# A fused retention and MLP kernel: batch 0's queries and keys loaded four tokens a partition by head pair

## The chip, the cores and the metric

The kernel runs on one core of a Trainium2 chip. The time is device microseconds of one launch; a kernel's time is the median of its runs. A profiled execution has a time of its own, and a span: from its first to its last instruction.

## The reference

```python
# q, k, v: (8, 8, 576, 64) float32   w_in: (512, 2048)   w_out: (2048, 512)
scores = q @ k.T / sqrt(64)                          # per batch and head
gamma  = 1 - 2 ** (-5 - h)                           # per head
ret    = scores * where(i >= j, gamma ** (i - j), 0)
x      = (ret @ v), heads side by side               # (8 * 576, 512)
out    = gelu_tanh(x @ w_in) @ w_out                 # (4608, 512)
```

The mask depends on the difference of positions alone, so the attention can be cut into chunks: scores inside a chunk of 128 tokens, and a 64 by 64 state per head that carries what came before.

## The kernel before

**Tiles.** A batch has 512 tokens in four chunks, and 64 tail tokens, which have a path of their own (`Tt`, `kqt`, `vt`). The number `s` is the half of 256 tokens, `hh` the half of four heads. `load_qkv(b, s, hh, key)` brings 256 KB into a tile of 128 partitions by 512 float32: partition p has tokens 2p and 2p + 1 of the half, for four heads, so each run in memory is 512 bytes. `cast_qk` (the copies all have line L232) makes float16 of it in the order token, head, feature, in `kq[:, s, hh, i, :]`, where i is 0 for keys and 1 for queries. `cast_v` (L241) does so for values and folds a decay into them.

**Attention of a batch.** `tr` transposes 128 by 128 blocks of `kq` on TensorE (L342) into a PSUM bank and copies them (L232 again) into `T`, whose index g = 2r + pp stands for token parity r and head pair pp. When its engine is written `S2`, ScalarE takes one half of the copy and VectorE the other. `score_mm` (L395) multiplies transposed keys and queries; `mask_sc` (L408, VectorE) applies the mask on the way out of PSUM, into `ret`. `state_mm` (L463) multiplies the natural keys in `kq` with the values; `scan` (L479, L483, VectorE) carries the state on from chunk to chunk, and `put` (L232) writes it into block-diagonal tiles `tbd`, which `tbd_zero` (L132) cleared. `values` (L510) is `ret` times values, `inter_mm` (L537) adds the state's part for chunk n = 2s + c, and `evac` (L550, VectorE) scales the sum into `x`.

**The MLP.** `up` (L598) and `up_half` (L684) multiply `w_in` and x, and ScalarE applies the gelu (L602, L690). `up_half(j, u)` needs half u of x alone, and all four row blocks of its column group of `w_in`, cast to float16 by `cast_w_in`. The down-projection (`product`, L740) forms seven products of mixed operands ("my" to "mz2") in place of eight; the sums and differences that they need are made by `mix_sa`, `mix_sc`, `mix_d` (L701, L709, L713), for the weights by `mix_w_out` (L323 to L331), and `settle` (L767) puts the results together. In the last two blocks (the tail rows of all batches, then batch 7), some up-projections go the same way (`pair_*`, with `forms_w` and `forms_x`).

**The order.** All loads go out on SP's queue, in the order of the `load_*` calls, from line 860 on. A load needs one of 12 slots, or a tile on loan (E, E2, E3, O, H); a slot comes free when the cast of what it held is issued in program order, and SP then waits for that cast. The order of all else is a list of units (mostly one up-projection or down-product each) and a plan: entries (unit, step), run after that unit, in the order of the list. The first ten units are empty, so all of batch 0's attention stands there. Each engine runs its own instructions in this order and waits at each for what it needs. `pads` gives the number of filler transposes or matmuls (L147, L149) that TensorE runs ahead of a step while it has nothing else, and `warm` (L138) fills its first microseconds.

Of the kernel before, what the change touches and what calls it, by code (L numbers as in the profile page):

```python
# [13 lines left out]
F16 = mybir.dt.float16  # L14
# [5 lines left out]
def kernel(  # L20
# [106 lines left out]

    tbd = [const.tile([128, NC, HP, 128], F16, name=f"tbd{i}") for i in range(2)]
# [56 lines left out]
    def load_qkv(b, s, hh, key, home=None):  # L185
        def one(home):
            t = ld(home)
            nc.sync.dma_start(  # L188
                out=t.rearrange("p (h e) -> p h e", h=4),
                in_=SRC[key][b, 4 * hh : 4 * hh + 4, 256 * s : 256 * s + 256, :].rearrange(  # L190
                    "h (p r) d -> p h (r d)", r=2
                ),
            )
            att[b][key, s, hh] = t

        todo.append((one, home))
        pump()
# [36 lines left out]
    def cast_qk(b, s, hh, key, eng):  # L234
        t = att[b].pop((key, s, hh))
        copy(eng, unperm(att[b]["kq"][:, s, hh, "kq".index(key), :]), perm(t))
        done(t)
# [99 lines left out]
    def tr(b, s, hh, i, eng):  # L337
# [3 lines left out]
        for g in range(4):  # L341
            nc.tensor.transpose(t[:, 128 * g : 128 * g + 128], a["kq"][:, s, hh, i, 128 * g : 128 * g + 128], ident)  # L342
        src = t[:, 0:512].rearrange("p (g t) -> p g t", g=4)
# [34 lines left out]
    def tr_tail_dma(b):  # L378
        a = att[b]
        nc.sync.dma_start_transpose(  # L380
            out=a["Tt"].rearrange("p i s t -> p (i s) t"),
            in_=a["kqt"].rearrange("p i c -> p (i c)"),
        )

# [463 lines left out]
    def add(plan, *entries):  # L848
# [12 lines left out]
    load_qkv(0, 0, 0, "q", None)  # L861
    load_qkv(0, 0, 1, "k", None)
    load_qkv(0, 0, 0, "v", None)
    load_qkv(0, 0, 1, "q", None)
    load_qkv(0, 1, 0, "k", None)
    load_qkv(0, 0, 1, "v", None)
    load_qkv(0, 1, 1, "k", None)
    load_qkv(0, 1, 0, "q", None)
    load_w_in(0, 3, E)
    load_qkv(0, 1, 1, "q", None)  # L870
    load_qkv(0, 1, 0, "v", None)
    load_w_in(0, 0, E)
    load_qkv(0, 1, 1, "v", None)
    load_w_in(0, 2, E)
    load_w_in(0, 1, E)
    load_w_in(1, 1, E2)
    load_w_in(1, 0, E2)
    load_w_in(1, 3, E2)
    load_w_in(2, 2, None)
    load_qkv(1, 0, 0, "k", None)  # L880
    load_w_in(1, 2, E2)
    load_w_in(2, 3, None)
    load_w_in(2, 0, None)
    load_qkv(1, 0, 1, "q", None)
    load_w_in(2, 1, None)
    load_qkv(1, 0, 0, "q", None)
    load_qkv(1, 0, 1, "k", None)
    load_w_in(3, 0, None)
# [3 lines left out]
    load_w_in(3, 2, None)  # L892
    load_qkv(1, 0, 1, "v", None)
    load_qkv(1, 1, 0, "k", O)
    load_qkv(1, 1, 1, "q", O)
    load_qkv(1, 1, 0, "q", O)
    load_qkv(1, 1, 1, "k", O)
# [5 lines left out]
    load_w_out(2, None)  # L903
    load_w_out(3, None)
    load_w_out(10, H)
    load_w_out(4, E3)
# [3 lines left out]
    load_w_out(13, H)  # L910
    load_w_out(7, E3)
    load_w_out(9, O)
# [3 lines left out]
    load_w_out(12, H)  # L916
    load_qkv(2, 1, 0, "q", None)
    load_qkv(2, 1, 0, "k", None)
    load_qkv(2, 0, 0, "k", None)
    load_qkv(2, 0, 0, "q", None)  # L920
# [8 lines left out]
    load_tail(0)  # L929
    load_qkv(3, 0, 0, "v", None)  # L930
    load_qkv(3, 0, 0, "k", None)
    load_qkv(3, 0, 0, "q", None)
# [13 lines left out]
        ("tr", 0, 1, 0, 0): 0,  # L946
        ("tr", 0, 1, 1, 0): 0,
        ("tr", 0, 1, 1, 1): 5,
        ("st", 0, 1, 0): 6,
        ("st", 0, 1, 1): 11,  # L950
        ("us", 0, 0): 0,
        ("us", 0, 1): 8,
        ("xs", 0, 0): 1,
        ("xs", 0, 1): 2,
# [3 lines left out]
        ("tr", 0, 0, 1, 0): 24,  # L958
        ("tr", 0, 0, 1, 1): 9,
        ("st", 0, 0, 0): 12,  # L960
        ("st", 0, 0, 1): 7,
        ("us1", 0, 0): 3,
        ("tr", 0, 1, 0, 1): 6,
        ("in", 0, 1): 12,
        ("us1", 0, 1): 1,
        ("in", 0, 2): 4,
# [6 lines left out]
    def turn():  # L973
# [7 lines left out]
    plan = add({},  # L981
        (0, L(tbd_zero, 0, G)),
        (0, L(cast_qk, 0, 0, 0, "q", G)),
        (0, L(cast_qk, 0, 0, 0, "k", G)),
        (0, L(mask)),
        (0, L(tr, 0, 0, 0, 1, A)),
        (0, L(cast_v, 0, 0, 0, G)),
        (0, L(tr, 0, 0, 0, 0, S2)),
        (0, L(score_mm, 0, 0, 0)),
        (1, L(cast_qk, 0, 0, 1, "k", V)),  # L990
        (1, L(tr, 0, 0, 1, 0, A)),
        (3, L(mask_sc, 0, 0, 1)),
        (5, L(tbd_zero, 1, G)),
        (0, L(cast_v, 0, 0, 1, G)),
        (1, L(mask_sc, 0, 0, 0)),
        (1, L(cast_qk, 0, 0, 1, "q", V)),
        (1, L(tr, 0, 0, 1, 1, V)),
        (3, L(state_mm, 0, [0])),
        (2, L(score_mm, 0, 0, 1)),
        (3, L(cast_qk, 0, 1, 0, "q", G)),  # L1000
        (0, L(cast_qk, 0, 1, 0, "k", G)),
        (3, L(scan, 0, 0)),
        (3, L(put, 0, 0, A)),
        (6, L(cast_qk, 0, 1, 1, "q", G)),
        (0, L(new_x, 0)),
        (4, L(scan, 0, 1)),
        (5, L(evac, 0, 0, 0)),
        (4, L(tr, 0, 1, 0, 0, V)),
        (3, L(values, 0, 0)),
        (4, L(tr, 0, 1, 0, 1, S2)),  # L1010
        (5, L(cast_qk, 0, 1, 1, "k", A)),
        (4, L(put, 0, 1, A)),
        (6, L(score_mm, 0, 1, 0)),
        (5, L(inter_mm, 0, 0, 1)),
        (5, L(evac, 0, 0, 1)),
        (8, L(cast_w_in, 0, 0, V)),
        (6, L(tr, 0, 1, 1, 0, A)),
        (7, L(mask_sc, 0, 1, 0)),
        (7, L(cast_v, 0, 1, 0, G)),
        (7, L(score_mm, 0, 1, 1)),  # L1020
        (6, L(tr, 0, 1, 1, 1, A)),
        (7, L(cast_v, 0, 1, 1, V)),
        (8, L(scan, 0, 2)),
        (7, L(state_mm, 0, [1])),
        (7, L(mask_sc, 0, 1, 1)),
        (8, L(put, 0, 2, V)),
        (8, L(cast_w_in, 0, 1, G)),
        (3, L(cast_w_in, 0, 3, A)),
        (9, L(cast_w_in, 0, 2, G)),
        (9, L(F0.up_half, 0, 0)),  # L1030
        (10, L(F0.up_half, 1, 0)),
        (8, L(values, 0, 1)),
        (9, L(evac, 0, 1, 0)),
        (12, L(cast_w_in, 1, 0, G)),
        (9, L(inter_mm, 0, 1, 1)),
        (15, L(cast_w_in, 2, 3, G)),
        (9, L(evac, 0, 1, 1)),
        (8, L(inter_mm, 0, 1, 0)),
        (8, L(turn)),
        (9, L(cast_w_in, 1, 3, A)),  # L1040
        (12, L(cast_qk, 1, 0, 0, "k", G)),
        (15, L(cast_qk, 1, 0, 1, "k", A)),
        (7, L(cast_w_in, 1, 2, A)),
        (11, L(scan, 0, 3)),
        (11, L(F0.mix_sa, 0, 2, V)),
        (14, L(F0.mix_sc, 0, 2, V)),
        (10, L(cast_w_in, 1, 1, V)),
        (10, L(cast_w_in, 2, 2, G)),
        (14, L(cast_w_in, 2, 1, A)),
        (10, L(cast_w_in, 2, 0, V)),  # L1050
        (19, L(F0.mix_sc, 2, 2, V)),
        (16, L(cast_qk, 1, 0, 1, "q", G)),
        (16, L(cast_qk, 1, 0, 0, "q", G)),
        (16, L(F0.mix_d, 0, 2, V)),
        (19, L(tr, 1, 0, 1, 0, V)),
        (18, L(cast_w_in, 3, 0, G)),
        (16, L(tr, 1, 0, 0, 0, S2)),
        (11, L(put, 0, 3, A)),
        (17, L(cast_w_in, 3, 2, G)),
        (19, L(tr, 1, 0, 1, 1, A)),  # L1060
        (20, L(F0.mix_sa, 2, 2, V)),
        (17, L(tr, 1, 0, 0, 1, S2)),
        (20, L(score_mm, 1, 0, 0)),
        (21, L(F0.mix_d, 2, 2, V)),
        (27, L(inter_mm, 1, 0, 0)),
        (21, L(cast_v, 1, 0, 1, G)),
        (22, L(mask_sc, 1, 0, 1)),
        (18, L(cast_w_in, 3, 1, A)),
        (16, L(cast_v, 1, 0, 0, G)),
        (21, L(mask_sc, 1, 0, 0)),  # L1070
        (18, L(cast_w_in, 3, 3, G)),
        (21, L(score_mm, 1, 0, 1)),
        (26, L(scan, 1, 1)),
        (22, L(state_mm, 1, [0])),
        (21, L(new_x, 1)),
        (26, L(cast_qk, 1, 1, 0, "k", G)),
        (22, L(scan, 1, 0)),
        (22, L(put, 1, 0, A)),
        (22, L(values, 1, 0)),
        (23, L(inter_mm, 1, 0, 1)),  # L1080
        (27, L(cast_v, 1, 1, 0, V)),
        (23, L(evac, 1, 0, 1)),
        (28, L(put, 1, 1, A)),
        (22, L(cast_qk, 1, 1, 1, "q", A)),
        (25, L(cast_qk, 1, 1, 0, "q", G)),
        (22, L(cast_qk, 1, 1, 1, "k", A)),
        (28, L(F0.mix_sa, 4, 2, V)),
        (28, L(F0.mix_sc, 4, 2, V)),
        (27, L(cast_v, 1, 1, 1, V)),
        (22, L(evac, 1, 0, 0)),  # L1090
        (25, L(tr, 1, 1, 0, 1, A)),
        (28, L(tr, 1, 1, 0, 0, V)),
        (26, L(tr, 1, 1, 1, 1, A)),
        (28, L(state_mm, 1, [1])),
        (28, L(F0.mix_d, 4, 2, V)),
        (28, L(tr, 1, 1, 1, 0, A)),
        (31, L(mask_sc, 1, 1, 0)),
        (31, L(mask_sc, 1, 1, 1)),
        (28, L(score_mm, 1, 1, 0)),
        (32, L(inter_mm, 1, 1, 1)),  # L1100
        (29, L(score_mm, 1, 1, 1)),
        (31, L(values, 1, 1)),
        (30, L(mix_w_out, 0, "sums", G)),
        (29, L(scan, 1, 2)),
        (29, L(put, 1, 2, A)),
        (31, L(inter_mm, 1, 1, 0)),
        (31, L(mix_w_out, 0, "sub", V)),
        (30, L(mix_w_out, 1, "copy", A)),
        (37, L(mix_w_out, 3, "add", G)),
        (31, L(mix_w_out, 1, "add", V)),  # L1110
        (32, L(mix_w_out, 2, "sums", G)),
        (31, L(mix_w_out, 1, "sums", G)),
        (32, L(evac, 1, 1, 0)),
        (33, L(evac, 1, 1, 1)),
        (33, L(mix_w_out, 3, "sub", V)),
        (37, L(mix_w_out, 7, "add", V)),
        (37, L(mix_w_out, 3, "sums", V)),
        (32, L(mix_w_out, 3, "copy", A)),
        (33, L(mix_w_out, 1, "sub", V)),
        (32, L(mix_w_out, 2, "add", G)),  # L1120
        (38, L(mix_w_out, 0, "copy", A)),
# [390 lines left out]
```

## Time and profile before

| what | us |
|---|---|
| median of 6 runs | 299.55 |
| lowest and highest run | 298.75, 301.22 |
| profiled execution | 299.48 |
| its span | 297.7 |
| TensorE busy in it | 289.1 |
| VectorE busy | 237.1 |
| ScalarE busy | 164.0 |
| GpSimd busy | 104.9 |

Instructions are told by engine (PE for TensorE, PEld for its weight loads, DVE for VectorE, ACT for ScalarE, POOL for GpSimd, SP for SyncE, which issues the DMAs) and by the line of the kernel. A tile of the form `a<-b` is written from b. Matmuls are pipelined, so the length of a row is not a matmul's share of the engine, and a busy TensorE includes filler. TensorE's granted clock is full in the whole span.

### The profile page before, as it was taken

How to read it: one execution, taken by the hardware profiler on the slowest of the kernel's cores; microseconds unless marked ns; L12 is line 12 of the kernel's file. 1: busy time of each engine (PE TensorE's matmuls, PEld its weight loads, DVE VectorE, ACT ScalarE, POOL GpSimd, SP SyncE). 2: the span in 40 equal slices, each digit the busy share in tenths (PEclk: the TensorE clock that was granted, in tenths of full speed). 3: DMA queues.
4: the chain of work that ended last, by engine and by line, in shares of the span. 5: the costliest groups of instructions: out<-in, count | busy, mean ns of one | idle time of the engine just before them, and what ended most of it. 6: DMA issues, size and time to landing. Idle time of an engine off the chain costs nothing.

```text
span 297.7 us, 8946 instructions
## 1 busy us (share of the span) xinstructions
PE 289.1 (97%) x3761; PEld 210.0 (71%) x3761; DVE 237.1 (80%) x442; ACT 164.0 (55%) x318; POOL 104.9 (35%) x136
## 2 busy tenths in 40 slices
PE   8979999999999999999999999999999999999994
PEld 6866477888885568655875587558754886787684
DVE  3795899999997995798568756899688198896793
ACT  7428798875556781665445554564445317605720
POOL 6743664545250433280064005699000000310050
PEclk9999999999999999999999999999999999999999
DMA  7999999858889999979994998482120002002204
GB/s 207 305 327 330 303 380 329 233 143 202 230 240 226 323 231 221 293 221 132 265 259 127 140 254 249 138 140 23 47 98 0 2 34 112 0 2 70 70 2 141
DMA packets 94711, 52.48 MB, mean 176 GB/s; under 512 B 38352, under 2 KB 88528, under 8 KB 94672
## 3 DMA queue, kind: packets, MB, share of 16 engines
q1 hardware_dynamic: 94336, 51.26, 65.5%
q10 hardware_dynamic: 336, 0.66, 0.8%
q8 instruction: 29, 0.48, 0.7%
q14 instruction: 10, 0.08, 0.1%
HBM read 36.70 MB, written 9.44 MB: 155 GB/s over the span
## 4 chain that ended last, share of the span: by engine, by line
PE 71%; DMA 12%; DVE 9%; SPq 3%; ACT 3%; issue 1%; POOL 0%; DVEq 0%; ACTq 0%
PE hp L598 26%; PE my L740 9%; PE mz L740 9%; PE mu L740 5%; PE mw L740 5%; PE mv L740 4%; PE hp L684 2%; PE py L628 2%; DMA loan<-in_q_dram 2%; SPq L188 2%; DMA ld<-in_moe_w_in_dram 2%; DMA ld<-in_v_dram 2%; PE xs L510 2%; DVE ret L408 2%; DVE ost L767 2%; DMA loan<-in_moe_w_in_dram 2%
## 5 line engine op out<-in xcount | busy, mean ns | idle before, releaser
L598 PE MATMUL hp<-x,w_in_sb 128*128 128x512 f16 x400 | 92.4, 379 | 0.6 <-ACT gT L602 0.5
L602 ACT ACTIVATE gT<-hp 128x512 f16<-128x512 f32 x108 | 63.8, 598 | 42.1 <-PE hp L598 41.1
L598 PEld LDWEIGHTS <-w_in_sb 128*128 128x128 f16 x432 | 40.9, 98 | 43.3 <-issue 1.0
L740 PEld LDWEIGHTS <-gT 128*128 128x128 f16 x576 | 55.7, 98 | 8.3 <-ACT gT L671 0.2
L232 POOL CAST kq<-ld 128x512 f16<-128x512 f32 x30 | 23.0, 769 | 60.6 <-DMA ld<-in_k_dram 45.9
L408 DVE TENSOR_TENSOR ret<-st,cm 128x512 f16<-128x512 f32 x64 | 39.9, 679 | 3.7 <-PE st L395 3.5
L241 POOL TENSOR_TENSOR cv<-ld,sc 128x512 f16<-128x512 f32 x28 | 30.3, 1093 | 29.1 <-DMA ld<-in_v_dram 28.9
L232 ACT CAST tbd<-ws 64x256 f16<-64x256 f32 x62 | 25.0, 403 | 25.2 <-DVE ws L483 21.7
L740 PE MATMUL my<-w_out_sb,gT 128*128 128x256 f16 x288 | 34.6, 273 | 0.0
L740 PE MATMUL mz<-w_out_sb,gT 128*128 128x256 f16 x288 | 34.4, 273 | 0.0
L713 DVE TENSOR_TENSOR gT<-gT 128x1024 f16<-128x1024 f16 x34 | 30.8, 918 | 0.2
L740 PEld LDWEIGHTS <-gsum 128*128 128x128 f16 x288 | 28.0, 98 | 3.5
L709 DVE TENSOR_TENSOR gsum<-gT 128x1024 f16<-128x1024 f16 x36 | 29.7, 828 | 0.5 <-ACT gT L602 0.5
L701 POOL TENSOR_TENSOR gdia<-gT 128x512 f16<-128x512 f16 x2 | 3.0, 1482 | 71.0 <-ACT gT L602 49.3
L550 DVE TENSOR_TENSOR x<-xs,gx 128x512 f16<-128x512 f32 x32 | 21.6, 682 | 4.7 <-PE xs L537 4.5
L701 DVE TENSOR_TENSOR gdia<-gT 128x512 f16<-128x512 f16 (+1 forms) x32 | 18.4, 574 | 4.9 <-ACT gT L671 2.5
L767 DVE TENSOR_TENSOR ost<-ost,mv 128x512 f32<-128x512 f32 x18 | 11.5, 678 | 11.6 <-issue 8.1
L684 PE MATMUL hp<-x,w_in_sb 128*128 128x256 f16 x160 | 18.9, 273 | 1.0 <-DVE x L550 0.9
L684 PEld LDWEIGHTS <-w_in_sb 128*128 128x128 f16 x160 | 15.3, 98 | 3.1 <-issue 1.3
L740 PE MATMUL mu<-w_out_sb,gsum 128*128 128x256 f16 x144 | 17.2, 272 | 0.2 <-DVE ret L408 0.2
L740 PE MATMUL mv<-w_out_sb,gsum 128*128 128x256 f16 x144 | 17.2, 273 | 0.0
L740 PE MATMUL mw<-w_out_sb,gdia 128*128 128x256 f16 x144 | 17.2, 273 | 0.0
(113 smaller groups left out, 405.6 us busy)
## 6 DMA issues: line engine op xcount, KB each, us to landing
ld<-in_k_dram SPq DMA_DIRECT2D x30, 256.0 KB, 5.0
ld<-in_q_dram SPq DMA_DIRECT2D x30, 256.0 KB, 5.4
ld<-in_v_dram SPq DMA_DIRECT2D x30, 256.0 KB, 5.5
out_dram<-ost SPq DMA_DIRECT2D x14, 512.0 KB, 4.5
loan<-in_moe_w_out_dram SPq DMA_DIRECT2D x12, 256.0 KB, 5.4
loan<-in_moe_w_in_dram SPq DMA_DIRECT2D x8, 256.0 KB, 6.0
ld<-in_moe_w_in_dram SPq DMA_DIRECT2D x8, 256.0 KB, 6.2
ld<-in_moe_w_out_dram SPq DMA_DIRECT2D x4, 256.0 KB, 5.2
```

The source lines that it names most:

```text
L232: (eng.copy if eng is nc.scalar else eng.tensor_copy)(out=out, in_=in_)
L241: eng.tensor_tensor(out=unperm(att[b]["v"][:, s, hh, :]), in0=perm(t), in1=sc[:, 8 * hh : 8 * hh + 8] .rearrange("p (r h) -> p r h", r=2) ...
L408: nc.vector.tensor_tensor(out=x.rearrange("p (a m) -> p a m", a=2), in0=st[hl].rearrange("p (a m) -> p a m", a=2), in1=cm.rearrange("p r s ...
L550: nc.vector.tensor_tensor(out=xb[b][:, :, 2 * s + c].rearrange("p s q i -> p q s i"), in0=att[b]["x", s][c].rearrange("p (q s i) -> p q s ...
L598: nc.tensor.matmul(hp, w_in_sb[:, ct, 128 * f : 128 * f + 128], x[:, :, ct, :], start=(ct == 0), stop=(ct == 3),)
L602: nc.scalar.activation(out=self.g(f // 2)[:, f % 2], in_=hp, func=AF.Gelu_apprx_tanh)
L684: nc.tensor.matmul(hp[:, 256 * h : 256 * h + 256], w_in_sb[:, ct, 256 * j + 128 * h : 256 * j + 128 * h + 128], xb[self.b][:, :, 2 * u : 2 ...
L701: e.tensor_tensor(out=self.sa[:, j : j + n], in0=g[:, :, 0, 0:256], in1=g[:, :, 1, 256:512], op=ALU.add)
L709: e.tensor_tensor(out=self.sc[:, j : j + n], in0=g[:, :, 0], in1=g[:, :, 1], op=ALU.add)
L713: e.tensor_tensor(out=g.rearrange("p j h c -> p j (h c)")[:, :, 256:768].rearrange("p j (h c) -> p j h c", h=2), in0=g[:, :, :, 0:256], in ...
L740: nc.tensor.matmul(t[u] if isinstance(t, list) else t[:, 256 * u : 256 * u + 256], lhs(j, slice(128 * u, 128 * u + 128)), w_out_sb[:, j, w ...
L767: nc.vector.tensor_tensor(out=out, in0=in0, in1=t, op=op)
```

## The change

Queries and keys of batch 0 (the set `R4`) are loaded with four tokens a partition for a pair of heads over all 512 tokens: runs of 1,024 bytes, and `s` now numbers the pair within the head half. The cast orders them by token and head. After the transposes, column p of block r is token 4p + r; two copies for each `tr`, which step through PSUM with an inner stride of 256 elements, put the tokens into the layout that `T` had. So `T` is as before, but the natural keys in `kq` are not: `back` transposes `T` to natural keys again, for `state_mm`. Scores of a head half now need the tiles of both pairs.

The loads, the pads and the plan are reordered for it, and the plan of batch 1 and of the last two blocks is changed as well.

```diff
+    R4 = {(0, "k"), (0, "q")}
 def load_qkv ... one(home):
+            if (b, key) in R4:
+                g = 2 * (2 * hh + s)
+                nc.sync.dma_start(
+                    out=t.rearrange("p (h e) -> p h e", h=2),
+                    in_=SRC[key][b, g : g + 2, 0:M0, :].rearrange("h (p r) d -> p h (r d)", r=4),
+                )
+                att[b][key, s, hh] = t
+                return
 def cast_qk
-        copy(eng, unperm(att[b]["kq"][:, s, hh, "kq".index(key), :]), perm(t))
+        o = att[b]["kq"][:, s, hh, "kq".index(key), :]
+        if (b, key) in R4:
+            copy(eng, o.rearrange("p (r h d) -> p r h d", r=4, h=2), t.rearrange("p (h r d) -> p r h d", r=4, h=2))
+        else:
+            copy(eng, unperm(o), perm(t))
 def tr
+        if (b, "kq"[i]) in R4:
+            src = t[:, 0:512].rearrange("p (q r s m) -> p s r m q", q=2, r=2, s=2)
+            for r in range(2):
+                e = (A, V)[r] if eng is S2 else eng
+                copy(
+                    e,
+                    a["T"][:, :, hh, i, 2 * r + s, :].rearrange("p s (m q) -> p s m q", q=2),
+                    src[:, :, r],
+                )
+            return
+    def back(b, s, hh, eng):
+        a = att[b]
+        t = bank("tr", F16)
+        pad(("bk", b, s, hh), t)
+        for r in range(2):
+            for pp in range(2):
+                o = 256 * r + 128 * pp
+                nc.tensor.transpose(t[:, o : o + 128], a["T"][:, s, hh, 0, 2 * r + pp, :], ident)
+        copy(eng, a["kq"][:, s, hh, 0, :], t[:, 0:512])
```

The loads of batch 0 before: k and q of (s, hh) = (0, 0), k (0, 1), v (0, 0), q (0, 1), k (1, 0), v (0, 1), k (1, 1), q (1, 0), a weight, q (1, 1), v (1, 0), a weight, v (1, 1), two weights. After: k, q (0, 0), k, q (1, 0), k, q (0, 1), q, k (1, 1), v (0, 1), v (0, 0), a weight, v (1, 0), v (1, 1), three weights.

The plan after, units 0 to 9, for the steps of batch 0 (arguments: batch, s, hh or chunk, k = 0 or q = 1, engine; A is ScalarE, V VectorE, G GpSimd):

```python
(0, cast_qk 0,0,0 q A) (0, cast_qk 0,0,0 k V) (0, cast_qk 0,1,0 q V) (0, tr 0,0,0,0 V) (0, cast_qk 0,1,0 k A) (0, mask)
(0, cast_qk 0,0,1 k A) (0, tbd_zero 0 G) (1, tr 0,0,0,1 V) (1, tr 0,1,0,0 V) (1, tr 0,1,0,1 S2) (1, cast_qk 0,1,1 q G)
(1, cast_qk 0,1,1 k G) (2, score_mm 0,0,0) (2, mask_sc 0,0,0) (2, back 0,0,0 V) (2, cast_qk 0,0,1 q G) (2, tr 0,0,1,0 S2)
(2, tr 0,0,1,1 A) (3, score_mm 0,1,0) (3, back 0,1,0 A) (3, tr 0,1,1,1 V) (3, mask_sc 0,1,0) (3, tr 0,1,1,0 A)
(3, cast_v 0,0,0 G) (3, cast_v 0,0,1 G) (4, score_mm 0,0,1) (4, mask_sc 0,0,1) (5, back 0,0,1 A) (5, state_mm 0,[0])
(5, scan 0,0) (5, values 0,0) (5, scan 0,1) (5, put 0,1 A) (5, evac 0,0,0) (6, score_mm 0,1,1) (6, put 0,0 A)
(6, mask_sc 0,1,1) (6, cast_w_in 0,3 A) (7, back 0,1,1 A) (7, cast_v 0,1,1 V) (7, cast_v 0,1,0 G) (7, state_mm 0,[1])
(7, scan 0,2) (7, put 0,2 S2) (7, values 0,1) (7, tbd_zero 1 G) (7, cast_w_in 1,0 1,3 1,2 A) (8, inter_mm 0,0,1)
(8, evac 0,0,1) (8, inter_mm 0,1,1) (8, inter_mm 0,1,0) (8, cast_w_in 0,1 0,0 G) (8, cast_w_in 1,1 A) (9, cast_w_in 0,2 G)
(9, evac 0,1,0) (9, evac 0,1,1) (9, up_half 0,0) (9, up_half 1,0), then units 10 and 11: up_half 0,1 and 1,1
```

Before, `up_half(0, 0)` stood at unit 9 ahead of `evac(0, 1, 0)`, and `evac(0, 0, 1)` at unit 5. In the last two blocks, `mix_d(0)` and `mix_sa(6)` move from GpSimd to VectorE, and some lists are sorted by unit.

## The prediction

> **What bounds the kernel now.** I read the page first (busy shares, slices, chain), then TensorE's waits, then the timeline of the first 28 us.
>
> The page: busy time; in slices of 7.4 us, TensorE, VectorE and DMA; the chain by engine.
>
> ```profile
> PE 289.1 (97%) x3761; PEld 210.0 (71%) x3761; DVE 237.1 (80%) x442; ACT 164.0 (55%) x318; POOL 104.9 (35%) x136
> PE   8979999999999999999999999999999999999994
> DVE  3795899999997995798568756899688198896793
> DMA  7999999858889999979994998482120002002204
> PE 71%; DMA 12%; DVE 9%; SPq 3%; ACT 3%; issue 1%; POOL 0%; DVEq 0%; ACTq 0%
> ```
>
> TensorE is nearly full from the fourth slice on, so a time is set by two things: when its dense stretch starts, and what it loses afterwards. The 12% of DMA in the chain lie before 46 us: the loads run without a pause, but that is not yet a loss of TensorE's. Its waits from 22.3 to 60 us say so (waiter, awaited: us in total, times, longest):
>
> ```profile
> PE hp L684 <- DVE x L550: 0.9, 1, 0.9
> PE us L463 <- POOL cv L241: 0.4, 1, 0.4
> PE xs L510 <- DVE ret L408: 0.3, 1, 0.3
> ```
>
> After the first line only 0.7 us are left to win before 60 us. That first line is the end of batch 0's attention. The timeline (start, length, engine, operation, idle before it and what ended it):
>
> ```profile
> 6.57 0.29 DVE L232 COPY T<-tr 128x256 f16<-128x256 f16 x1 [3.58 <-ACT T L232]
> 7.21 1.51 PE L147 MATMUL tr<-ident,wz 128*128 128x128 f16 x24
> 9.71 0.43 DVE L232 COPY T<-tr 128x512 f16<-128x512 f16 x1 [0.77 <-PE tr L342]
> 10.64 1.29 DVE L408 TENSOR_TENSOR ret<-st,cm 128x512 f16<-128x512 f32 x2 [0.51 <-PE st L395]
> 12.35 0.82 ACT L232 CAST tbd<-ws 64x256 f16<-64x256 f32 x2 [2.78 <-POOL kq L232]
> ...
> 19.88 1.04 PE L684 MATMUL hp<-x,w_in_sb 128*128 128x256 f16 x8
> 20.97 1.29 DVE L550 TENSOR_TENSOR x<-xs,gx 128x512 f16<-128x512 f32 x2
> 22.31 2.78 PE L684 MATMUL hp<-x,w_in_sb 128*128 128x256 f16 x24 [0.92 <-DVE x L550]
> ```
>
> TensorE's first useful up-projection is at 19.88 us (8 matmuls, a step of 0.87 us); it then waits for x and is dense from 22.31 us. Had those 8 stood in line with the rest, the stretch would begin at 22.31 - 0.87 = **21.44 us**. That is the number to beat. TensorE is "busy" earlier too, but much of that is filler (L147, L149: 24 of them took 1.51 us). What decides is VectorE's queue, busy 4.83 of 5 us before 20 us, while the loads ran at (stretch; busy us of PE, PEld, DVE, ACT, POOL; clock; DMA share; GB/s):
>
> ```profile
> 5.00:10.00 5.00, 5.00 (x95) 4.51 (x92) 2.54 (x6) 2.02 (x5) 1.66 (x3) 1.00 1.13 301
> 15.00:20.00 5.00, 4.44 (x125) 3.82 (x126) 4.83 (x10) 1.53 (x3) 1.96 (x3) 1.00 1.02 345
> ```
>
> The first row is q, k, v in runs of 512 B; the second has mostly weights in runs of 2 KB.
>
> **What the Trainium skill says.** "VectorE: DVE Perf Modes", section "Mode 2×_1P": two 16-bit elements a cycle need elements next to each other in memory. The trace agrees for today's PSUM copies: 512 elements take 422 ns, 256 take 291 ns, so 0.51 ns an element, where the 32-bit masks (L408) take 1.04 if the same fixed 0.15 us is taken off their 684 ns. "DMA: Bandwidth & Descriptors", section "Why small descriptors are slow (HBM only)": a fixed 3 cycles a packet beside its 32-byte beats; so 19 cycles for 512 B and 35 for 1 KB, 8% less a byte. The two rows above (301 and 345 GB/s) go the same way. "TensorE: Matmul & The Clock Gate", section "Part 4: PE-mode transpose": a transpose ends in PSUM and needs a copy after it; here every L342 group has its L232 copy.
>
> **The change, part by part.**
>
> *Loads.* Eight 256 KB loads go from 512 packets to 256. By the 8% above and the two rows I take 0.08 us off 0.86 us each: -0.65 us on the stream after the eighth, -0.3 us at the fourth. In the DMA issue view the fourth load now is issued at 2.32 and lands 5.0 us later, at 7.3 us; it will be at about 7.0. Bounds: nothing, or -1.1 us if the dip in DMA traffic between 3.6 and 5.2 us goes too. Nothing after 22 us waits for the stream for more than the 0.36 us of one GpSimd value cast, so on TensorE I count these savings only through the fourth load. On SP the first 16 loads are the same set in another order, all into free slots or loans, so none waits there; the later ones keep number and size and are costed at nothing while the stream stays ahead of TensorE. If that cover went, the 0.36 us would grow by what they come late.
>
> *What the first scores need.* A tile now holds one head pair over all 512 tokens, so scores of either token half need four loads, not two. VectorE, which reaches its first transpose copy at 6.57 us today, has the cast of the fourth load second in its queue: it starts at 7.0, and the copies behind it wait though their transposes are done.
>
> *PSUM copies.* Each of 8 `tr` calls makes two copies of 256 elements whose inner step is 256 elements. Two elements a cycle are excluded by the first citation, so 0.15 + 256 x 1.04 ns = **0.42 us** (estimate), as much as a whole 512 today. Between 0.29 us (still two a cycle) and 0.60 us (a strided PSUM read that costs more, no row shows it). Ten fall to VectorE and six to ScalarE (0.37 us each, the row of its 256 copies). Today VectorE has two whole and two half copies. Back to back a VectorE row starts about 0.08 us before the last one ends (two of 684 ns cover 1.29), so a step is 0.34 us.
>
> *Casts.* The first two leave GpSimd, which zeroes `tbd` (L132) until 4.4 us; the same three or so stay there (0.61 us each, from the seventh landing at about 9.4), then three value casts of 1.04 us from 11.9 and the weights from 16.8 to 18.6 us, all before their users above. ScalarE's first cast waits for its table load, until 5.5 us, which the fourth landing hides.
>
> *`back`.* Four times four transposes (0.22 us of TensorE each time, in place of filler) and a copy of 512: one on VectorE (0.43 us), three on ScalarE (0.59 us). State products now wait for them.
>
> *VectorE's queue placed in order.* Cast of q at 7.0, six half copies and the mask (L116), 8 steps of 0.34: 9.75; the half behind ScalarE's ends 10.2. Scores 0.4 us, so masks of (0, 0) from 10.7 to 12.0, `back` to 12.3. Meanwhile TensorE runs 23 fillers (1.3 us) before the next transposes; ScalarE's half follows at 12.5, VectorE's at 12.95 (today's first line above shows that a shared copy runs one half after the other). Then q of (1, 1): 13.9 to 14.6. Four mask products of 0.6: 17.0. Two scans, 1.3 us: 18.25. An evacuation, the last masks and a value cast: 0.6 + 1.2 + 0.6 = 20.6.
>
> *The chain that ends last.* `put` of n = 1 and 0 waits on ScalarE for the second scan at 18.3. Four copies of 0.41 with overlap 0.09, 1.3 us: 19.65; behind them a weight cast, 0.53: 20.2; behind that `back` (1, 1), 0.59: **20.8**. State products 0.35: 21.15; scan 2 with its sum, 0.9: 22.1; `put` 0.3: 22.4; evacuation of chunk 1, 0.69: 23.1; products of `inter_mm` stand in TensorE's queue ahead: **23.4 us** for the first up-projection. All of x follows at 24.9, early enough for the two calls that need it.
>
> So 23.4 - 21.44 = **+2.0 us**. Afterwards the waits of 0.4 and 0.3 us have like ones in the new order (masks of batch 1): 0. Pads: 129 before, 127 after: 0. The tail's two moved GpSimd operations and sorted lists: 0; the new VectorE queue there (4.4 us of mixes from 282.65) is done at 287, ahead of the last three products. If this cover went, only the 0.4 us step of one mix would show.
>
> The profiled execution took 299.48 us (span 297.7 and 1.78 around it), the median is 299.55: both 299.5 here. **299.5 + 2.0 = 301.5 us.** A measurement of this kernel tells about 0.5%, 1.5 us, from no change.
>
> **The rivals.** *No slowdown: the copies stay at two a cycle and the dip goes with the packets.* Ten copies at 0.29 take 1.2 us off VectorE's queue, the fourth landing at 6.2 another 0.8: a start at 21.4, 299.5 us; with the 0.7 us of later waits gone also, 298.8. It decides from a copy under 0.37 us together with a landing before 6.7. For it: the dip shows that the stream is not at its rate yet; against it: the adjacency rule, and no row of a strided copy. *One of the two only*: 300.3 to 300.7, no change. *Copies cost more than one a cycle*: at 0.60 us, +1.6: 303.1. *The loads gain nothing* (a packet costs by its bytes): +0.3: 301.8. *A second loss after 25 us*, since four weight casts stand on ScalarE ahead of the first gelu: if up-projections run out of PSUM banks, +1 to 2: 303. The tail of this reaches past 304.
>
> **How the numbers follow.** Start at 23.4 with copies at one a cycle: 0.55, its own range 300.7 to 302.6. Dearer copies or a second loss: 0.15. One favour: 0.20. Both: 0.07, and 0.03 for more than both. Slower by over 0.5% is most of the first and all of the second: 0.66. Within 0.5%: the rest of the first, one favour, most of both: 0.28. Faster: 0.06. Leaving out about a tenth on each side: 299.1 to 304.3.
>
> **What would show it.** Right: strided L232 copies of 128x256 on VectorE at 0.40 to 0.45 us; 1 KB packets; first dense L684 near 23.4 us, its wait on x or on what feeds it (ScalarE's `back` copy before the state products); waits between 25 and 60 us still under 1 us. Wrong: copies at 0.29; a first L684 before 21.9; or a span that grows by something after 60 us, which I hold to be unchanged.

## The result and the profile after

| | us |
|---|---|
| after, median (28 runs) | 301.79 (299.89 to 305.1) |
| before, median (63 runs) | 299.84 (297.94 to 304.14) |
| after to before | **1.0066, 95% interval 1.0051 to 1.0081** |
| profiled execution of after | 302.41, its span 300.6 |

The change costs 2.0 us. The page of the kernel after: busy time, slices of 7.5 us, the chain by engine.

```profile
PE 291.2 (97%) x3775; PEld 212.6 (71%) x3775; DVE 234.2 (78%) x450; ACT 167.8 (56%) x328; POOL 96.1 (32%) x128
PE   8869999999999999999999999999999999999995
DVE  3786789989998896889667766689878288886774
PEclk9997999999999999999999999999999999999999
DMA  6998999669979999794999699654030003002204
PE 82%; DVE 7%; ACT 6%; DMA 2%; issue 1%; SPq 0%; DVEq 0%; ACTq 0%
```

TensorE is as full as before from the fourth slice on. The second and third slices fell from 9 to 8 and from 7 to 6, and in the fourth (22.5 to 30 us) the granted clock is 0.7, which it was nowhere before. The loads have left the chain (DMA 12% to 2%): they are not what the start waits for. Two of TensorE's waits in the whole span:

```profile
PE us L500 <- ACT kq L241: 2.2, 1, 2.2
PE st L432 <- DVE T L241: 1.2, 2, 0.7
```

From 22.3 to 60 us only this is left, where before stood 0.9, 0.4 and 0.3:

```profile
PE xs L547 <- issue: 0.2, 1, 0.2
PE xs L547 <- DVE ret L445: 0.2, 1, 0.2
PE xs L574 <- ACT tbd L241: 0.2, 1, 0.2
```

The timeline of the start (start, length, engine, operation, idle before it and what ended it):

```profile
7.21 0.43 DVE L241 CAST kq<-ld 128x512 f16<-128x512 f32 x1 [2.53 <-DMA ld<-in_q_dram]
8.55 1.74 DVE L241 COPY T<-tr 128x256 f16<-128x256 f16 x5
10.68 1.29 DVE L445 TENSOR_TENSOR ret<-st,cm 128x512 f16<-128x512 f32 x2 [0.40 <-PE st L432]
...
18.02 0.87 DVE L520 TENSOR_TENSOR ws<-vs,gt 128x256 f32<-128x256 f32 x1
18.98 1.65 ACT L241 CAST tbd<-ws 64x256 f16<-64x256 f32 x4 [2.72 <-DVE ws L520]
20.65 0.62 ACT L241 CAST w_in_sb<-loan 128x512 f16<-128x512 f32 x1
21.17 0.58 ACT L241 COPY kq<-tr 128x512 f16<-128x512 f16 x1
21.80 0.32 PE L500 MATMUL us<-cv,kq 64*64 64x64 f16 x16 [2.24 <-ACT kq L241]
...
23.80 1.06 PE L574 MATMUL xs<-T,tbd 128*128 128x128 f16 x8
24.47 0.69 DVE L587 TENSOR_TENSOR x<-xs,gx 128x512 f16<-128x512 f32 x1 [0.96 <-PE xs L574]
25.82 2.34 PE L721 MATMUL hp<-x,w_in_sb 128*128 128x256 f16 x16
```

The chain is the predicted one: scan, put, weight cast, copy of `back` (1, 1), state. But the first up-projection comes at 25.82 us, not at 23.4. The stretches around it (us; busy us of PE, PEld, DVE, ACT, POOL; clock; DMA share; GB/s) show a part that the prediction did not have:

```profile
22.00:23.00 1.00, 0.76 (x49) 0.50 (x37) 0.73 (x2) 0.00 (x0) 0.00 (x0) 1.00 1.11 330
23.00:24.00 1.00, 1.00 (x16) 1.00 (x13) 0.41 (x2) 0.85 (x3) 0.00 (x0) 0.64 1.12 325
24.00:25.00 1.00, 1.00 (x13) 1.00 (x11) 0.53 (x1) 1.00 (x3) 0.00 (x0) 0.50 1.21 314
25.00:26.00 1.00, 1.00 (x11) 0.98 (x10) 0.16 (x1) 0.63 (x2) 0.14 (x1) 0.50 1.09 342
26.00:27.00 1.00, 1.00 (x8) 0.75 (x6) 0.93 (x2) 0.00 (x0) 0.47 (x1) 0.66 0.97 337
```

After its wait of 2.24 us TensorE ran at half clock, from about 23.3 to 26.7 us (0.72 + 1 + 1 + 0.68 = 3.4 us of halves).

**Two kinds of executions.** Each execution's mean clock tells whether it had such a stretch: 3.4 us at half are 1.7 of 300, a mean of 0.994. Of 48 executions of this kernel (27 of the 28, and 21 of the repeat below), 25 kept the clock (mean 0.997 and more; median 301.04 us) and 23 had lost it (0.992 to 0.994, one 0.987; 302.41). Of 190 of the kernel before on the chips of the experiments, 189 kept it. Single disturbed executions are left out of these counts, and of those below. So the loss of 2.0 us is about 1.2 at full clock, and 1.4 more in half of the executions. Resampling the executions puts this 1.2 between 0.6 and 1.7, and this 1.4 between 1.0 and 2.0. Below, "at full clock" is the median of the first group, set against that of the kernel before on the same chip (299.96, 299.84, 299.62 and 299.85 in the four sets). These groups are small, 6 to 15 executions, and resampling moves their medians by 0.5 to 1 us; differences of a few tenths at full clock are hints, and the profiles have to carry them.

### The profile page after: what moved, and what is told of

It reads as the page before. It is cut to its first block, busy times and chain, and to the rows that moved or that the text cites. A ratio compares the mean times of both kernels' runs of the same rounds, so it can differ in the third digit from the quotient of the medians.

```text
span 300.6 us, 8979 instructions
## 1 busy us (share of the span) xinstructions
PE 291.2 (97%) x3775; PEld 212.6 (71%) x3775; DVE 234.2 (78%) x450; ACT 167.8 (56%) x328; POOL 96.1 (32%) x128
## 4 chain that ended last, share of the span: by engine, by line
PE 82%; DVE 7%; ACT 6%; DMA 2%; issue 1%; SPq 0%; DVEq 0%; ACTq 0%
PE hp L635 26%; PE my L777 10%; PE mz L777 9%; PE hp L721 6%; PE mu L777 5%; PE mv L777 5%; PE mw L777 5%; PE xs L547 2%; PE xs L574 2%; PE py L665 2%; ACT tbd L241 2%; PE st L432 2%; DMA ld<-in_q_dram 2%; DVE ret L445 2%; ACT gT L639 1%; DVE T L241 1%
## 5 line engine op out<-in xcount | busy, mean ns | idle before, releaser
L241 POOL CAST kq<-ld 128x512 f16<-128x512 f32 x26 | 18.7, 720 | 65.6 <-DMA ld<-in_k_dram 49.1
L254 POOL TENSOR_TENSOR cv<-ld,sc 128x512 f16<-128x512 f32 x28 | 31.0, 1119 | 26.8 <-DMA ld<-in_v_dram 26.8
L746 DVE TENSOR_TENSOR gsum<-gT 128x1024 f16<-128x1024 f16 x35 | 28.4, 813 | 2.3 <-ACT gT L727 1.8
L750 DVE TENSOR_TENSOR gT<-gT 128x1024 f16<-128x1024 f16 x36 | 27.8, 791 | 0.1
L738 DVE TENSOR_TENSOR gdia<-gT 128x512 f16<-128x512 f16 (+1 forms) x33 | 16.8, 508 | 4.8 <-ACT gT L708 2.5
L241 ACT CAST kq<-ld 128x512 f16<-128x512 f32 x28 | 17.0, 616 | 2.2 <-DMA ld<-in_k_dram 1.3
```

What stands on the lines that cost most here:

```text
L241: (eng.copy if eng is nc.scalar else eng.tensor_copy)(out=out, in_=in_)
L254: eng.tensor_tensor(out=unperm(att[b]["v"][:, s, hh, :]), in0=perm(t), in1=sc[:, 8 * hh : 8 * hh + 8] .rearrange("p (r h) -> p r h", r=2) ...
L738: e.tensor_tensor(out=self.sa[:, j : j + n], in0=g[:, :, 0, 0:256], in1=g[:, :, 1, 256:512], op=ALU.add)
L746: e.tensor_tensor(out=self.sc[:, j : j + n], in0=g[:, :, 0], in1=g[:, :, 1], op=ALU.add)
L750: e.tensor_tensor(out=g.rearrange("p j h c -> p j (h c)")[:, :, 256:768].rearrange("p j (h c) -> p j h c", h=2), in0=g[:, :, :, 0:256], in ...
```

## The experiments

All were timed in five rounds against the kernel before on the same chip: medians of before 299.96 us (beside the repeat, the filler, both moves, the late start), 299.88 (values first, adjacent columns, 512-byte loads, last two blocks), 299.66 (fewer fillers, split copies) and 299.96 (moved fillers, `back` alone).

### The kernel after again

No edit. It gives the full-clock profile that the others are held against.

> The changed kernel itself, beside the others on the same chip. Theory A (two costs: a start that is later by VectorE's and ScalarE's queue, and TensorE's clock, which falls to half after the 2.2 us wait for the last copy of natural keys): about 301.8 us, with executions of clock 1.000 near 300.5 and of clock 0.993 near 302.3. Rival B (the queues alone; the clock in the profile is by chance): 301.8 us, without any order by clock.

Measured: 301.5 us, ratio 1.0051 (1.0029 to 1.0074). 14 executions at full clock, 301.12 (1.2 above before); 7 not, 302.81. The profiled one (span 299.2) kept its clock: state wait 1.5 us instead of 2.24, first up-projection at 24.72 us, the first eight products of `inter` in 0.61 us where they took 1.06 at half clock.

### More filler under the wait

```diff
-        ("us1", 0, 1): 0,
+        ("us1", 0, 1): 38,
```

> The changed kernel with 38 filler matmuls (about 2.1 us) between the two halves of the state products of chunks 2 and 3, where TensorE waits 2.2 us; nothing else is changed, and no engine's queue gets shorter. Theory A: the clock stays at 1.000 in every execution, the first dense up-projection comes near 24.7 us in place of 25.8, and the time falls by 1.0 to 1.6 us, to about 300.5. Rival B: filler moves nothing that is waited for: no change, or up to 0.2 us slower.

Measured: 303.89 us, ratio 1.0125 (1.0084 to 1.0166). All six executions kept the clock (0.998 to 1.000), as the clock's part of my theory wanted, but the time rose: 2.8 us above the kernel after at full clock. The profile, of one execution, shows half of this at a place far from the edit. ScalarE issues three stores at 280 us; first the repeat of the kernel after, then this kernel:

```profile
278.39 1.38 ACTq L828 DMA_DIRECT2D out_dram<-ost  x3
```

```profile
279.91 2.80 ACTq L828 DMA_DIRECT2D out_dram<-ost  x3
282.76 0.59 ACT L683 COPY q<-pv 128x512 f32<-128x512 f32 x1 [2.39 <-PE hp L635]
284.12 0.60 PE L665 MATMUL py<-xf,wf 128*128 128x256 f16 x4 [1.41 <-DVE q L684]
```

The issues took 2.80 us instead of 1.38, the copy stood behind them, and TensorE lost 1.41 us waiting for its result. One of the three issues took 1.85 us instead of 0.43. It ran while a 16,384-byte transfer of the instruction queue was under way, 280.21 to 281.88 us, and ended 0.36 us after it. The queue table of this stretch (queue: packets, MB, share of 16 engines):

```profile
q10 hardware_dynamic: 91, 0.25, 60.3%
q8 instruction: 1, 0.02, 6.1%
```

In the repeat the next such transfer came at 282.97 us, 3.2 us after the issues. The 38 fillers lengthen TensorE's instruction list, and with it the times of these transfers change; so the edit may well have caused this, though no run moved a transfer alone. Another 0.5 us is at the first up-projection (25.21): the 38 fillers end at 22.6, later than the copy that they were to cover (21.57 in the repeat), and the rest, 1.0 us, builds up before 121 us. Filler kept the clock in all six, but it stands in TensorE's own queue ahead of the chain.

### `back` (1, 1) early, and both late value casts on GpSimd

```diff
         (5, L(back, 0, 0, 1, A)),
+        (5, L(back, 0, 1, 1, A)),
-        (7, L(back, 0, 1, 1, A)),
-        (7, L(cast_v, 0, 1, 1, V)),
-        (7, L(cast_v, 0, 1, 0, G)),
+        (3, L(cast_v, 0, 1, 0, G)),
+        (3, L(cast_v, 0, 1, 1, G)),
```

> The changed kernel with two steps moved: the last natural-key copy (head half 1, token half 1) right behind the one before it, ahead of ScalarE's state copies and weight cast; and the value casts of token half 1 both on GpSimd ahead of its clearing of the second tbd, so VectorE loses one. Theory A: no 2.2 us wait, clock 1.000, second scans from 20.7 us instead of 22.2, first up-projection near 23.0 us; 2.8 us earlier, of which the end keeps 1.5 to 2.5 us: 299.3 to 300.3, level with the kernel before. Rival C (the copies that step through PSUM set VectorE's end, so its queue is as late as before): at most 0.7 us faster than the changed kernel.

Measured: 300.81 us, ratio 1.0041 (1.0015 to 1.0068); at full clock 300.25 (13 executions), 0.3 above before where the kernel after is 1.2 above; 7 executions lost the clock. The state's wait is gone (all 32 products at 18.95 us), first up-projection 23.36. In the place of the wait TensorE now stops in the middle of the value products:

```profile
19.23 0.44 PE L547 MATMUL xs<-ret,cv 64*64 64x128 f16 x17
...
21.28 0.41 PE L547 MATMUL xs<-ret,cv 64*64 64x128 f16 x15 [1.61 <-DVE tbd L241]
```

The trace names VectorE's put, which ended at 21.20. But the value products read nothing of it. The next runs look for the cause.

### `back` (1, 1) early alone

The edit above without its last four lines.

> The kernel after, with the reading back of keys (1,1) moved to unit 5 and nothing else. My prediction's step (its copy stands behind put and weight cast on ScalarE and releases the state): the state's wait for ScalarE goes; it is then held by VectorE's value cast, which stands behind two masks: 20.43 to 21.10 in the kernel after at full clock, less about 0.4 for the earlier queue. State at 20.7 to 21.2 instead of 21.62, first up-projection 24.0 to 24.3 instead of 24.72, 0.3 to 0.6 below the kernel after at full clock (301.1 to 301.2): 300.6 to 300.9, ratio 1.003 to 1.005. Rival (the copy alone is the wait): state at 19.0 to 19.6, as in the kernel with both edits, then ratio 1.003 or less.

Measured: 301.75 us, ratio 1.0052 (1.0034 to 1.0069); at full clock 300.79, 0.9 above before. The state starts at 21.45 us instead of 21.62, now released by the other late input:

```profile
21.45 0.32 PE L500 MATMUL us<-cv,kq 64*64 64x64 f16 x16 [1.28 <-DVE cv L254]
```

So the copy of `back` and VectorE's value cast were late together; taking away the copy alone is worth 0.2 us at the state and 0.3 in time. The first up-projection came at 24.56. VectorE's four masks began 0.27 us later in this profile than in the repeat (14.98 and 14.71), so the edit may be worth a little more.

### The value products written ahead of the put

From the kernel with both edits, `values` (0, 1) moves in the plan ahead of `scan` 2 and its put.

> The early-back kernel (reading back of half (1,1) moved to unit 5, both value casts of tokens 512 to 1023 on GpSimd), and besides the values products of those tokens written ahead of scan 2 and its put. The order of instructions on each engine stays; only what the products can be made to wait for changes. Theory W (TensorE's 1.6 us in the middle of L547 is a wait for the put written ahead of it): the wait goes, TensorE goes on at 20.0 instead of 21.28, first up-projection matmul about 22.5 instead of 23.36, no execution loses its clock, time 0.8 below the early-back kernel at full clock: 299.5 to 300.0, ratio 0.998 to 1.001. Theory F (TensorE stands at its 352nd matmul whatever is written there; the kernel after also pauses there, 0.43 us put down to issue): nothing changes, wait 1.3 to 1.7 us, first matmul 23.3 to 23.5, 300.3 to 301, ratio 1.004.

Measured: 302.15 us, ratio 1.0066 (1.0039 to 1.0093); at full clock 300.55, 0.7 above before, and 10 of 21 executions without it. Every engine's order stayed, and so did the stop: 2.2 us, before the same product, the 352nd of TensorE's list. It ended at 23.39 us, 0.62 after the put (22.48 + 0.29). It is no wait for VectorE, whatever the row says; theory W fell.

In nine kernels the stop is at the 352nd product or, 128 earlier, the 224th. A product and its weight load are two instructions, so the distance is 256 of them. On a queue of kind "instruction" the traces have 29 transfers of 16,384 bytes, and 30 in the two kernels with 38 and 54 fillers more: 2 times 3,775 products are 29.5 blocks of 256, 2 times 3,813 are 29.8. The count goes with TensorE's list. "Runtime: NRT & Kernel Launch" of the Trainium skill, section "Instruction fetch mechanics", says that an engine's instructions come in blocks of 16 KiB, 256 instructions, by a DMA queue of its own, and calls the cost of a boundary mostly hidden. The size agrees. The times in the packet records are the evidence here: from the start of that transfer to TensorE's going on it is 2.42 us in the kernel after (20.22, 22.64), 2.50 in its repeat, 2.47 in the kernel with both edits (18.81, 21.28), 2.65 here (20.74, 23.39). Over all twelve stops it is 2.42 to 2.67; in the four profiles of the changed kernels that pass the 352nd product without a stop, 2.54 us or more had gone by. In the kernel after, the stop lay behind the state's wait and cost 0.24 us, in the repeat 0.43.

### Fewer fillers ahead of that boundary

From the kernel with both edits; 21 fillers less put all value products ahead of the 352nd:

```diff
-        ("st", 0, 1, 1): 8,
+        ("st", 0, 1, 1): 0,
-        ("us", 0, 1): 8,
+        ("us", 0, 1): 0,
-        ("xs", 0, 0): 5,
+        ("xs", 0, 0): 0,
```

> The early-back kernel with 21 filler products fewer ahead of the values products of tokens 512 to 1023 (8, 5 and 8 in three places), so that those products all lie ahead of TensorE's 352nd matmul. Theory I (TensorE stands at a fixed place of its instruction list until a 16 KB instruction transfer, begun about 2.5 us before, is there): the 1.6 us in the middle of L547 goes, values end near 20 us, the stop moves into the ten fillers ahead of inter, which wait for the put (21.2) anyway; first up-projection at 22.4 to 22.7 instead of 23.36, 0.7 to 0.9 below the early-back kernel's 300.25 at full clock: 299.4 to 299.7, ratio 0.998 to 1.001. Theory R (it waits for VectorE's result, whatever is written ahead): the stop stays inside L547, now with 15 of 32 left, time as the early-back kernel, 300.3, ratio 1.004. Fewer fillers may cost clock: then over 1.005, with mean clock below 0.995 in most executions.

Measured: 301.01 us, ratio 1.0033 (1.0009 to 1.0056); at full clock 300.02 (7 executions), 0.4 above before, no different from the kernel with both edits within the noise; 15 had lost the clock. The stop moved by exactly the 21 products, out of L547 and into the fillers behind it:

```profile
20.13 0.41 PE L547 MATMUL xs<-ret,cv 64*64 64x128 f16 x15 [0.39 <-DVE ret L445]
20.48 0.51 PE L150 MATMUL us<-wz 128*128 128x128 f16 x6
22.39 0.59 PE L150 MATMUL us<-wz 128*128 128x128 f16 x4 [1.40 <-issue]
```

Fillers wait for nothing, so this is the list and not the data: theory I. The transfer is the one packet of its kind in 19.7 to 21.1 us (queue: packets, MB, share of 16 engines), where the loads fill the engines:

```profile
q1 hardware_dynamic: 593, 0.45, 103.3%
q8 instruction: 1, 0.02, 5.3%
```

It started at 19.85 us, so 2.54 to the going on. But the gain I expected did not come: this transfer started later than in the kernel with both edits (18.81), so the stop ended later as well. What sets its start I could not find; it lay between 18.1 and 20.7 us over the kernels.

### The first three copies split between ScalarE and VectorE as well

```diff
-        (0, L(tr, 0, 0, 0, 0, V)),
+        (0, L(tr, 0, 0, 0, 0, S2)),
```

and so for `tr` (0, 0, 0, 1) and (0, 1, 0, 0).

> The kernel with 21 fillers fewer, and the copies of the first three transposed tiles of tokens 0 to 511 split between ScalarE and VectorE (one half copy each), which takes three 0.37 us copies off VectorE's queue. From the kernel with contiguous copies, where 0.9 us taken off the copies before 10.3 us came through to the scans: scans end 0.6 to 1.1 earlier, first up-projection at 21.5 to 22.0, 0.5 to 1.0 below the kernel with fewer fillers: 298.6 to 299.2, ratio 0.995 to 0.998, faster than before. Rival (ScalarE's casts of the next keys get behind the copies, or the instruction transfer is now what is late): 0 to 0.3, ratio 0.998 to 1.001.

Measured: 300.47 us, ratio 1.0019 (0.9996 to 1.0041); at full clock 299.38 in 11 executions, 0.2 below before; the other 11 at 300.79. In the profile the transfer started at 18.10 us and nothing was seen of it:

```profile
20.32 0.80 PE L150 MATMUL us<-wz 128*128 128x128 f16 x10
20.96 0.74 PE L574 MATMUL xs<-T,tbd 128*128 128x128 f16 x8
...
22.16 3.66 PE L721 MATMUL hp<-x,w_in_sb 128*128 128x256 f16 x32
```

### Thirteen fillers moved to TensorE's next gap

```diff
-        ("xs", 0, 1): 0,
+        ("xs", 0, 1): 13,
-        ("tr", 0, 0, 1, 0): 23,
+        ("tr", 0, 0, 1, 0): 10,
```

> The kernel with split copies, with 13 of the 23 fillers that TensorE runs near 11 us moved to the place ahead of the values products of tokens 512 to 1023 (17.7 us), where TensorE stood 0.8 us; the number of instructions up to there stays. Theory C (short waits between tiny products from 17.7 us on are what costs half of the executions their clock): at most 2 in 10 executions below 0.996, median falls by 0.5 to 1.0 to 299.4 to 299.9, ratio 0.998 to 1.001. Theory T (the clock goes when the instruction transfer is late and TensorE then stands over a microsecond, whatever runs before): the share stays at about half, ratio 1.001 to 1.003. Harm: if the shorter fill at 11 us lets the clock go earlier, over 1.004.

Measured: 300.56 us, ratio 1.0015 (0.9982 to 1.0047); at full clock 299.21 (7), 0.6 below before, otherwise 300.86 (7). The share that loses its clock stayed at half, so the wait of 0.8 us that these fillers cover is not by itself what costs it; stops of 0.57, 0.39 and 0.93 us are left in the profile. In the profile the stop is there again, after the sixth filler (0.93 us, to 21.00; transfer 18.41). As they are, this and the last kernel cannot be told from the kernel before.

### Copies of adjacent columns

```diff
-            src = t[:, 0:512].rearrange("p (q r s m) -> p s r m q", q=2, r=2, s=2)
+            src = t[:, 0:512].rearrange("p (r s m q) -> p s r m q", q=2, r=2, s=2)
```

> The kernel after, with the two half copies out of each transposed 128 x 512 tile of batch 0 reading adjacent columns; the tokens then stand in another order, so the output is not the reference's. Theory 'the strided copies on VectorE are what the start lost': ten VectorE copies fall from 415 ns to about 295, 1.2 us of its queue ahead of the scans, first up-projection matmul 0.8 to 1.2 earlier than in the kernel after at full clock (24.72 to about 23.7), time 1 below it, ratio at most 1.003. Theory 'the queue behind the scans (put, weight cast, copy of back(1,1) on ScalarE, value cast on VectorE) and the clock are what was lost': the copies give 0.3 at most, the 1.5 to 2.2 us wait of the state stays, ratio 1.004 to 1.006. In between, both hold in part.

Measured: 301.31 us, ratio 1.0039 (1.0015 to 1.0063); at full clock 300.19 (13), 0.35 above before; 8 had lost it. VectorE's ten copies to 25 us (group, count, busy us, mean ns, idle before), of the kernel after and of this one:

```profile
L241 DVE COPY T<-tr 128x256 f16<-128x256 f16 x10 | 3.7, 415 | 1.3 <-PE tr L355 0.6 <-ACT T L241 0.6
```

```profile
L241 DVE COPY T<-tr 128x256 f16<-128x256 f16 x10 | 2.3, 284 | 1.4 <-PE tr L355 0.8 <-ACT T L241 0.6
```

131 ns each, 1.3 us in all, and the state came 1.16 us earlier (20.46 instead of 21.62). ScalarE's six such copies took 376 ns in both. The time at full clock points the same way, 0.8 of the 1.2 us lost, but that difference alone is within its noise. The wait itself did not shrink:

```profile
PE us L500 <- ACT kq L241: 1.5, 1, 1.5
```

With this wait, as long as in the repeat, this profiled execution did lose its clock (half from 21.1 us, 3.4 us of halves again), and its first up-projection came at 24.88.

### Loads in runs of 512 bytes

The branch for `R4` in `load_qkv` is switched off. The casts keep the pattern of after, unlike what the expectation says, so the tokens land in another order; the first cast on VectorE takes 0.43 us either way.

> The kernel after, but the eight loads of queries and keys of batch 0 and their casts in the pattern of before (four heads, two tokens a partition, runs of 512 bytes); the rest as after, so that wrong tokens are used and the output is not the reference's. My prediction's step (1 KB runs are worth 0.65 us of the stream and 0.3 us at the 4th load): first VectorE cast at 7.45 instead of 7.2, DMA rate from 5 to 10 us 300 to 305 GB/s instead of 331, first up-projection 0.2 to 0.3 later, time +0.2 to +0.5 over the kernel after. Rival (the stream's rate carries the whole start, 10 per cent of 20 us): +1.5 to +2. Rival (hidden): 0.

Measured: 301.56 us, ratio 1.0057 (1.0038 to 1.0076); at full clock 301.23, 1.4 above before where the kernel after is 1.2 above. The rate from 5 to 10 us fell from 328 GB/s in the repeat to 295:

```profile
5.00:10.00 5.00, 4.52 (x65) 4.38 (x64) 2.73 (x9) 2.49 (x6) 0.00 (x0) 1.00 1.14 295
```

VectorE's first cast started at 7.26 us in both. The first up-projection came at 24.42, 0.3 earlier than in the repeat and not later. The 1 KB runs moved bytes faster by a tenth, and the time moved by no more than its noise.

### The last two blocks as before

Lists of the last two blocks from the kernel before.

> The kernel after with the operation lists of the last two blocks as before (two mixes on GpSimd, orders of before). My prediction's step (the lists cost nothing): same time as the kernel after within 0.3. Rival (the new lists gave back the 0.4 us by which the kernel after catches up in the last 100 us): +0.4, to be seen as a span from the mark at 199 us to the end longer by 0.4.

Measured: 302.28 us, ratio 1.0055 (1.0028 to 1.0083); at full clock 301.06 (6 executions), 1.2 above before as the kernel after. In the profile the stretch from 199 us to the end is 0.08 us longer than in the repeat. The lists cost and give nothing that these runs can tell.

### The kernel before, started late

```diff
         ("in", 0, 2): 4,
+        ("hp", 0, 0, 1, 0): 54,
```

> The kernel before with 54 filler matmuls (3.0 us) at the start of the second up-projection, behind the wait for x, so that TensorE's dense stretch begins 3.0 us later; all else is unchanged. Theory D (a late start is partly given back, since in the kernel before TensorE meets small waits for VectorE, GpSimd and loads later on, which a start 3 us later no longer meets): the time grows by 1.0 to 2.0 us. Rival E (TensorE is full, so a late start goes through whole): it grows by 2.8 to 3.0 us.

Measured: 303.49 us, ratio 1.0107 (1.0069 to 1.0145). It was to tell whether later stages give a late start back. The time rose by 2.1 to 4.3 us, more than theory D's 1 to 2, but the executions lie from 301.46 to 305.89, so it is inconclusive on how much. In the profile the dense stretch begins 3.33 us late (1.16 of it there before the fillers), 2.55 late at the up-projections near 50 us, then a wait of 1.2 us for VectorE's copies brings it to 3.5 at 66 us, and from 99 to 262 us the same products start 3.2 late, so little was given back. The long issue of stores near 280 us (2.65 us here) costs 1.3 more.

## Why the prediction was right, step by step

The time (301.5 against 301.79) and the sign were right; the sum behind them was right only by luck. At full clock the first up-projection came 1.3 us later than summed (24.72, not 23.4), the clock added 0.7 us on average, and 1.8 us came back later, where the prediction had nothing: two losses and a return that nearly cancel.

- **Copies, 0.42 us each: right.** Measured 415 ns; with adjacent columns 284. The statement of "VectorE: DVE Perf Modes", section "Mode 2×_1P", on adjacent elements held for reads of PSUM with a step of 256 elements.
- **VectorE's queue placed in order: right to the masks, then short.** Half copies to 10.3 (10.2 said), masks 10.7 to 12.0 (the same), masks end at 17.1 (17.0). The second scan ended at 18.9 instead of 18.25: its last row took 0.87 us where 0.42 is usual (0.45 in the repeat, whose scans ended at 18.7).
- **The chain that ends last: right in its order, 1 us short in its sizes.** Four puts took 1.65 us, so without the overlap that was counted on, not 1.3; the weight cast began only then; the copy of `back` ended at 21.75, not 20.8. Also, `back` was held to be the only release; the value cast ended at 21.28, and with `back` early alone it held the state to 21.45. From the state to the first up-projection the repeat took 3.10 us with a stop of 0.43 for the instruction list, which was not in the sum; without a stop there (the profile with the last blocks as before) it was 2.69, as predicted (2.6).
- **The clock: missing.** Filler and `inter` products at half speed are 1.4 us in half of the executions. I had read that the clock was full in the whole span before (it is from 4.3 us on, see the end), and did not ask what the new wait of 2 us would do to it.
- **"Loads: -0.3 us at the fourth": too large.** The landing came about 0.1 earlier (first cast at 7.21), and the run with 512-byte loads, whose first cast came at the same 7.26 us as the repeat's, shows no gain in time. The rate fell by more than the 8% that was estimated (328 to 295 GB/s), but the queue behind it hid this.
- **"Afterwards 0": wrong.** At full clock the first up-projection is 24.72 - 21.44 = 3.3 us behind the number to beat, the span only 1.5. Between the dense start and 92 us 1.4 come back: for the same work, less idle (0.43 instead of 1.08 us), and less busy time, 0.4 us of it in the same 404 products near 69 to 92 us (23.31 us, not 23.75). 0.4 more come back after 198 us. The kernel with both edits and the one with split copies show a like return (1.9 behind at the start, 0.2 in the span; 0.7 behind, 0.2 ahead). In the lists of before a start 3.3 us late was still 3.2 late at 262 us. That points to the order lists from 20 to 90 us, which the change re-sorted; that they do it was not tried. For the last blocks the prediction's 0 holds (301.06 with the lists of before, at full clock), so the 0.4 us after 198 us is not theirs and stays open.

Of the rivals, "one of the two only" (300.3 to 300.7) is near what adjacent copies give at full clock, 300.2. The favour from the loads that the first rival wanted besides did not show.

## What to carry to other kernels

When a step is moved onto a chain that TensorE waits for, price the clock with the wait: here, with stops of 1.4 to 2.2 us, half of the executions had 3.4 us at half speed, 0.7 us on average, about what the strided copies cost. A stop of TensorE that stays at the same instruction number whatever is written there is its instruction list; move fillers, and see whether it moves with the count. A layout change that buys longer DMA runs and pays with strided copies gains only if the loads, and not the queue behind them, hold the first consumer.

## What the runs showed of the hardware that was not expected

- **The clock.** "TensorE: Matmul & The Clock Gate", section "What's actually happening", describes a free-running activity window of about 3.4 us and half clock after one idle window; its section "Why this matters for your kernels" asks for no gaps over about 3 us. The half-clock stretches measured here last 3.4 us each in four profiles, as the page has it. But they came with stops of 2.24, 2.21, 1.53 and 1.40 us, with small products around them, and stops of 1.80, 1.61, 1.59, 1.50 and 1.28 us in five other profiles had none after them. So the length of the stop does not decide it.
- **Its phase.** At the start TensorE runs at half clock too, in both kernels, until a moment that differs between executions: 4.0 to 7.1 us in the fourteen profiles, 4.33 in the kernel before. It can be seen in the spacing of fillers and transposes, 107 ns and then 56. Four transposes of the kernel after, ahead of and behind that moment (6.21 us):

```profile
5.19 0.63 PE L355 MATMUL tr<-ident,kq 128*128 128x128 f16 x4
6.52 0.39 PE L355 MATMUL tr<-ident,kq 128*128 128x128 f16 x4
```

  In all four profiles the later half clock began 17.1 us after that moment, which is five times 3.41 us (6.21 and 23.28 us; 6.30 and 23.37; 4.84 and 21.91; 4.01 and 21.07). So the clock changed on a grid of 3.41 us that each execution places anew. Counted on this grid, TensorE stood still for 1.56 to 2.29 us of the fifth window where it lost the clock, and for at most 1.59 us of any window where it did not; the stop of 1.80 us lay across an edge. This fits a window that runs free, and would make the loss in half of the executions a matter of phase; no run moved the phase alone.
- **The instruction list** can stop TensorE for 0.2 to 2.2 us while loads fill the DMA engines: 2.4 to 2.7 us from the start of a 16,384-byte transfer to its first product.
- **Issuing three stores** on ScalarE's queue took 1.38 or 1.39 us in twelve profiles and 2.80 and 2.65 in the two of the kernels with more fillers than before or after. In these two alone an instruction transfer of 16,384 bytes was under way (280.21 to 281.88 us, 280.04 to 281.55), and the slow issue ended 0.36 us after it in both; in the twelve the next one started 2.5 us or more after the issues. That the transfer held the issue is not shown: in the first of the two profiles an issue on SyncE's queue at 296.68 us, during another transfer, took 0.39 us. The copy behind the stores came late and cost TensorE 1.3 to 1.4 us.
